# Windowed attention and an MLP in one kernel: the first two blocks of all four pairs of sequences first, the MLP in nine chunks of four blocks, v from the second block on by GpSimd's queue

## The chip, the cores and the metric

The kernel runs on one core of a Trainium2 chip. The metric is the device time of one execution in microseconds (us). The profile comes from one more such execution, in which the hardware recorded every instruction and every DMA packet; its times count from the start of its span.

## The reference

Attention over a window of 128 positions with a slope on the distance for each head, then a normalised two-layer MLP with a residual. Eight sequences of 576 positions, eight heads of 64, model width 512, hidden width 2048, all in float32:

```python
scores = scale * np.matmul(q, k.transpose(0, 1, 3, 2))
mask = (rel >= 0) & (rel < window)             # rel = position of q - position of k, window = 128
scores = np.where(mask, scores + bias[None], -1000000000.0)   # bias = -slope[head] * |rel|
attn = softmax(scores)
x = np.matmul(attn, v)                         # heads side by side: 8 x 576 x 512
xn = (x - mu) / np.sqrt(var + 1e-06) * g_ln
out = x + np.maximum(xn @ w_ch1, 0.0) @ w_ch2
```

## The kernel before

**Blocks.** The 8 x 576 positions are cut into 36 blocks of 128. Two sequences (a pair) make nine blocks (`PERIOD`); the middle one holds the end of one sequence and the start of the other. A block needs its own k and v and those of the block ahead of it in its pair; the first block of a pair (r = 0) needs only its own, and costs half. In the kernel before, block i is simply the i-th of the 36, so the four pairs follow each other.

**Attention of one block** (`attention(i)`). q and k come in as float32, are cast to fp16, turned so that the head dimension lies on the partitions (`qkt`), and multiplied (line 725, the tile `sc`, two halves of four heads each). ScalarE takes the exponential from `sc` into `probs` (773). For the first blocks (`i < BY_BIAS`) TensorE has added the slopes and the mask to `sc` beforehand, by multiplying `sid` with a table of distances (741); for the others VectorE multiplies `probs` with a table of masks (780), which ScalarE makes once (437). TensorE multiplies `probs` with `vx` (797); v has a column of ones, so the sums come with it. VectorE then does, in this order: reciprocal of the sums (814), `xb` = the normalised half (818) for both halves, the mean (851), `xs` = (xb - mean) * g (858), and the statistics (839, 845). `xs` is turned into `xt`, by TensorE (872, copied out by 880 or 882) for `i < X_BY_DMA` and by a transposing DMA on SP's queue (887) for the others.

**Three ways for q and k.** The blocks named in `SPANS` and the ones behind them come two at a time: one DMA on SP's queue (459) takes two positions at once, 512 bytes in a row, 1024 packets for the eight heads of two blocks; casts (619, 621) into `qs16`, `ks16`; four 32-bit transposes for each half of the heads (639); copies into `qkt` of both blocks (648, 650). `BY_HALVES` names the spans that are loaded and cast in two halves of four heads. Other early blocks come by 256-byte rows on SP's queue (364), and from `LOAD_CAST` on a DMA on GpSimd's queue casts on the way (473), and `qkt` is made by a transposing DMA on SP's queue (702) from `QK_BY_DMA` on. v of the blocks below `V_CAST` comes by SP's queue (364) and is cast by an engine (591, 593); from there on GpSimd's queue casts it on the way (473).

**MLP** (`mlp(c)`). The blocks are grouped in chunks; chunk c multiplies its `xt` with the first weights (919: 16 products `A` of four matmuls, as wide as the chunk has columns), applies relu (929, 931), and multiplies with the second weights (947: for each block 16 matmuls of 512 columns), then `ot` = product * rstd + xb (955) and out (963). The weights come in eight DMAs of 1 MB each on GpSimd's queue, casting: four for the first (536), four for the second (538). `W_AFTER` ties each to a point in the order of the loads.

**What sets the order.** A planner written in the kernel (`Plan.run`) lists all tasks with assumed costs and lays each on an engine by priority. The tables `PICK` (which engine), `PRI` (shifts of priority) and `HOLD` (earliest times) steer it. Its result is one fixed order of instructions on each engine and queue, and each engine works through its own in order; what the planner assumed does not hold anything back on the chip, only the order and the semaphores do. Where the planner sees TensorE idle before `WARM`, it fills the gap with matmuls on zeros (986) in whole numbers.

Rings (`Ring`) give the k-th user of a tile its buffer: buffer k modulo n, and the first write waits for the readers of user k - n.

Of the kernel before, what the change touches and what calls it, by code (L numbers as in the profile page):

```python
# [10 lines left out]
FP16 = mybir.dt.float16  # L11
# [15 lines left out]
class Ring:  # L27
    def __init__(self, tiles):
        self.tiles, self.first, self.readers = tiles, {}, {}

    def __getitem__(self, k):
        return self.tiles[k % len(self.tiles)]
# [7 lines left out]
    def link(self):  # L40
        n = len(self.tiles)
        for k, tasks in self.first.items():
            for t in tasks:
                t.deps += self.readers.get(k - n, [])


class Plan:
# [8 lines left out]
    LANDING = {"DMA SP": (0.7, 1.3), "DMA ACT": (0.7, 1.3), "DMA POOL": (2.1, 1.4)}  # L56
    LAST_OF_RUN = 1.0
# [6 lines left out]
    def ring(self, tiles):  # L64
        r = Ring(tiles)
        self.rings.append(r)
        return r
# [28 lines left out]
    def rates(self, queues):  # L96
        on = [q for q, x in queues.items() if x]
        if "DMA POOL" in on and len(on) > 1:
            a, b = (0.92, 0.17) if len(queues["DMA POOL"]) > 1 else (0.7, 0.4)
            return {q: a if q == "DMA POOL" else b / (len(on) - 1) for q in on}  # L100
        return {q: 1.0 / len(on) for q in on}
# [125 lines left out]
def kernel(  # L227
# [10 lines left out]
    nc = tc.nc  # L238
# [13 lines left out]
    CHUNKS = [3, 2, 3, 4, 4, 4, 4, 4, 4, 4]  # L252
# [15 lines left out]
    LEAD = 1.6  # L268
    WARM = 22.0
    TABLE_AFTER = 4  # L270
    STATS_LEAD = 10.0
    MIX_AFTER = 4
    SPLIT = 4
    LOAD_CAST = 9
    V_CAST = 5
    BY_HALVES = [0, 2, 5]
    HALVED = []
    SPANS = [0, 2, 5, 7]
    SLACK = (0, 0.2, 0)
    PICK = {('xt', 0): 'ACT', ('xt', 8): 'ACT DVE', ('cv', 5): 'ACT', ('cv', 0): 'POOL', ('ev', 8): 'ACT', ('ev', 1): 'DVE ACT', ('ev', 3): 'ACT', ('ck', 8): 'ACT', ('cq', 5): 'ACT', ('ev', 5): 'DVE', ('ck', 2): 'POOL', ('ck', 7): 'POOL ACT', ('cq', 6): 'POOL', ('cq', 2): 'POOL ACT', ('xt', 6): 'ACT', ('cq', 8): 'POOL', ('xt', 5): 'ACT', ('cv', 7): 'POOL ACT', ('cv', 3): 'ACT', ('xt', 3): 'DVE', ('ev00', 4): 'ACT', ('cs1', 1): 'POOL ACT', ('cs0', 0): 'POOL DVE', ('ev10', 3): 'ACT', ('xt', 2): 'DVE', ('cq', 3): 'POOL', ('cs0', 8): 'ACT', ('ev01', 8): 'DVE ACT', ('ev10', 8): 'DVE ACT', ('ev11', 5): 'ACT', ('cs0', 2): 'DVE', ('cq', 4): 'POOL', ('ev00', 8): 'DVE', ('ev01', 0): 'DVE ACT', ('cv', 8): 'POOL ACT', ('ev11', 0): 'ACT', ('cv', 4): 'POOL ACT', ('ev01', 6): 'ACT', ('cv', 6): 'POOL ACT', ('ev10', 5): 'ACT', ('cs1', 4): 'POOL', ('ev', 0): 'DVE', ('cv', 2): 'POOL ACT', ('ev00', 2): 'DVE ACT', ('ev00', 7): 'ACT', ('ev10', 2): 'ACT', ('xt', 1): 'ACT DVE', ('ev11', 8): 'DVE', ('xt', 4): 'DVE', ('ev00', 1): 'DVE ACT', ('cv', 1): 'POOL ACT', ('ev01', 7): 'DVE ACT', ('ev11', 6): 'DVE ACT', ('cq', 1): 'ACT', ('ev01', 4): 'DVE', ('cs0', 5): 'POOL', ('ev', 7): 'ACT', ('xt', 7): 'ACT DVE', ('ev', 9): 'ACT', ('cv', 9): 'POOL', ('cq', 11): 'POOL ACT', ('cs1', 9): 'POOL ACT', ('ev00', 10): 'ACT', ('eva', 5): 'ACT', ('cka', 9): 'ACT', ('cv', 11): 'POOL ACT', ('cqa', 10): 'DVE', ('ckb', 10): 'ACT', ('ck', 10): 'ACT', ('ev00', 5): 'ACT', ('ckb', 3): 'DVE', ('evb', 5): 'DVE', ('ev', 11): 'DVE', ('ev01', 2): 'DVE ACT', ('ckb', 6): 'ACT', ('eva', 11): 'DVE', ('cqb', 7): 'POOL DVE ACT', ('cka', 1): 'POOL DVE ACT', ('ev00', 3): 'ACT', ('cq', 0): 'ACT', ('ev01', 5): 'DVE', ('cqb', 5): 'DVE', ('ev10', 4): 'DVE ACT', ('ev01', 9): 'ACT', ('cqa', 8): 'ACT', ('ev10', 10): 'DVE', ('evb', 4): 'DVE ACT', ('cqb', 8): 'POOL ACT', ('cs0', 9): 'POOL DVE', ('cka', 3): 'POOL', ('cqa', 2): 'DVE', ('cka', 8): 'ACT', ('cqa', 5): 'POOL DVE ACT', ('cq', 7): 'POOL', ('ck', 1): 'POOL', ('cka', 0): 'POOL ACT', ('cqa', 7): 'ACT', ('ev10', 11): 'ACT', ('cqa', 4): 'ACT', ('ev11', 11): 'DVE', ('eva', 10): 'DVE ACT', ('ev11', 4): 'DVE', ('eva', 3): 'DVE', ('ev11', 2): 'DVE', ('cqa', 6): 'POOL', ('cqa', 9): 'POOL ACT', ('cqa', 11): 'POOL DVE ACT', ('ev', 2): 'DVE ACT', ('cs0', 4): 'POOL ACT', ('ckb', 11): 'DVE', ('ckb', 2): 'POOL DVE ACT', ('ck', 5): 'POOL', ('cs1', 8): 'ACT', ('ev01', 10): 'DVE ACT', ('ev', 10): 'DVE ACT', ('cq', 10): 'POOL', ('eva', 4): 'DVE', ('cv', 10): 'POOL', ('ev', 6): 'DVE ACT', ('ck', 11): 'ACT', ('cs1', 11): 'POOL ACT', ('cqb', 1): 'DVE', ('ckb', 7): 'DVE', ('ev11', 1): 'DVE ACT', ('ck', 4): 'POOL ACT', ('cka', 11): 'DVE', ('ckb', 0): 'POOL ACT', ('cs1', 0): 'POOL DVE', ('eva', 7): 'DVE', ('cs0', 11): 'POOL ACT', ('evb', 8): 'DVE ACT', ('ev10', 6): 'DVE', ('eva', 2): 'DVE', ('cqb', 2): 'ACT', ('cq', 9): 'POOL ACT', ('ev10', 9): 'DVE ACT', ('ev10', 0): 'DVE ACT', ('evb', 6): 'DVE ACT', ('eva', 8): 'ACT', ('cqa', 3): 'POOL ACT', ('ck', 9): 'ACT', ('evb', 3): 'DVE ACT', ('cs0', 1): 'DVE', ('cqb', 9): 'POOL DVE ACT', ('cqb', 0): 'POOL', ('evb', 2): 'ACT', ('evb', 1): 'ACT', ('cqb', 6): 'DVE', ('eva', 9): 'ACT', ('evb', 10): 'ACT', ('cqb', 11): 'DVE', ('cka', 10): 'POOL', ('ck', 6): 'POOL ACT', ('ckb', 1): 'POOL', ('ev10', 7): 'ACT', ('cs1', 7): 'ACT', ('ev01', 3): 'DVE', ('cs0', 7): 'POOL', ('cs0', 6): 'POOL DVE', ('cs1', 3): 'DVE', ('cka', 2): 'POOL ACT', ('cqa', 1): 'POOL ACT', ('ev01', 1): 'ACT', ('cs0', 10): 'POOL ACT', ('cka', 4): 'ACT', ('ev00', 6): 'DVE', ('xt', 10): 'DVE', ('cqb', 3): 'POOL DVE ACT', ('evb', 0): 'DVE ACT', ('ev00', 0): 'ACT', ('xt', 9): 'ACT', ('ev11', 7): 'DVE', ('cqb', 4): 'POOL DVE ACT', ('ev00', 9): 'DVE', ('ev00', 11): 'DVE ACT', ('ckb', 9): 'POOL ACT', ('ev11', 3): 'DVE ACT', ('ev01', 11): 'DVE', ('evb', 7): 'DVE ACT', ('ckb', 4): 'POOL ACT', ('ckb', 5): 'POOL ACT', ('cs1', 5): 'ACT', ('cs0', 3): 'POOL DVE', ('cka', 7): 'POOL', ('ev11', 9): 'DVE', ('cka', 5): 'ACT', ('cqb', 10): 'POOL', ('cs1', 6): 'POOL DVE', ('eva', 6): 'DVE', ('cs1', 10): 'POOL ACT', ('eva', 1): 'DVE', ('evb', 9): 'DVE ACT', ('ev10', 1): 'ACT', ('eva', 0): 'DVE', ('cka', 6): 'POOL ACT', ('ev11', 10): 'ACT', ('ev', 4): 'ACT', ('ck', 3): 'POOL ACT', ('cs00', 0): 'POOL ACT', ('cs10', 3): 'DVE', ('cs01', 10): 'ACT', ('cs11', 6): 'POOL', ('cs00', 9): 'POOL', ('cs01', 11): 'POOL', ('cs11', 9): 'ACT', ('cs00', 6): 'POOL DVE', ('cs11', 3): 'POOL DVE', ('cs01', 7): 'POOL', ('cs01', 8): 'POOL DVE', ('cs10', 11): 'POOL ACT', ('cs00', 8): 'DVE', ('cqa', 0): 'ACT', ('cs00', 2): 'POOL', ('cs01', 6): 'DVE', ('cs10', 4): 'DVE', ('cs10', 10): 'POOL ACT', ('cs00', 4): 'POOL', ('ck', 0): 'ACT', ('cs11', 5): 'DVE', ('cs11', 2): 'POOL', ('cs11', 8): 'DVE', ('cs01', 1): 'POOL', ('cs01', 4): 'POOL DVE', ('cs00', 1): 'POOL DVE', ('cs11', 0): 'POOL', ('ckb', 8): 'DVE', ('cs10', 9): 'POOL ACT', ('cs01', 9): 'POOL ACT', ('cs00', 10): 'POOL', ('cs01', 2): 'POOL', ('cs00', 5): 'POOL', ('cs11', 11): 'ACT', ('cs00', 3): 'POOL ACT', ('cs10', 1): 'ACT', ('cs01', 3): 'POOL', ('cs11', 1): 'DVE', ('cs11', 10): 'POOL DVE', ('cs11', 4): 'ACT', ('cs10', 6): 'POOL ACT', ('cs11', 7): 'ACT', ('cs10', 0): 'DVE', ('cs10', 5): 'ACT', ('cs10', 7): 'POOL'}  # L280
    PRI = {'T7.1': -4.2, 'A1.13': 6.1, 'rc0.8': -3.5, 'B4.0': 5.4}
    HOLD = {'mkb5': 43.12, 'v8.i': 46.02, 'nm0.7': 54.13, 'cT0.01': 7.07, 'cT5.10': 33.76, 'qs0.0.i': 1.25, 'g.i': 0.8, 'sid1': 4.85, 'mreg00': 28.48, 'z1': 31.56, 'r0.3': 28.11, 'r0.11': 36.69, 'rc1.8': 61.94}
    BY_BIAS = 5
    MASK_AT = 5
    QK_BY_DMA = 9
    X_BY_DMA = 12
# [7 lines left out]
    def ring(name, n, shape, dt):  # L294
        return plan.ring([sb(f"{name}{i}", shape, dt) for i in range(n)])
# [53 lines left out]

    def where(i):  # L350

        b0, r = 2 * (i // PERIOD), i % PERIOD
        if r < 4:
            return [(0, P, b0, P * r)]
        if r == 4:
# [23 lines left out]
    for t in vx.tiles:  # L379
        nc.vector.memset(t[:, :, D:VD], 1.0)  # L380
# [646 lines left out]
```

## Time and profile before

| | |
|---|---|
| Time, median of 8 executions (lowest, highest) | 320.58 us (319.49, 320.94) |
| The profiled execution: its time, its span | 320.02 us, 318.2 us |
| First matmul, end of the last | 1.07 us, 314.84 us |
| TensorE busy | 309.5 us, 2526 matmuls |
| of them the MLP's (lines 919 and 947) | 136.1 + 135.7 us, 640 + 592 |
| of them on zeros (line 986) | 8.0 us, 76 |
| VectorE, ScalarE, GpSimd busy | 185.5, 164.7, 98.7 us |
| First product of the MLP starts | 23.73 us |
| Landings of the four parts of the first weights | 22.09, 28.19, 34.94, 41.18 us |

A matmul's busy time is longer than the time that it keeps TensorE from the next, because matmuls overlap in the array. So work on TensorE is counted here by the time from one start to the next: 216 ns for 512 columns, 162 for 384, 109 for 256.

### The profile page before, as it was taken

What the parts mean: (1) busy time and instruction counts of PE and PEld (TensorE: products, weight loads), DVE (VectorE), ACT (ScalarE), POOL (GpSimd) and SP (SyncE); (2) the same over time, 40 slices, a digit from 0 to 9 for tenths busy, and PEclk for the clock granted to TensorE, in tenths of its full rate; (3) what the DMA queues carried; (4) which work ended last, traced back from release to release, by engine and by line L of the source; (5) the groups of instructions that cost most, each with busy time, mean ns of one, the idle gap of its engine ahead of it and who ended that gap; (6) DMA issues with size and microseconds to landing.
All of it is one profiled execution on the core that took longest, in us unless ns stands there. A gap on an engine that the chain in (4) does not pass through costs nothing.

```text
span 318.2 us, 6461 instructions
## 1 busy us (share of the span) xinstructions
PE 309.5 (97%) x2526; PEld 175.8 (55%) x2526; DVE 185.5 (58%) x511; ACT 164.7 (52%) x269; POOL 98.7 (31%) x131
## 2 busy tenths in 40 slices
PE   8988899999999999999999999999999999999995
PEld 7766676556655545554555555555555455445543
DVE  3679368865599648564866486548664866111012
ACT  2869776445656743474257425742575257305600
POOL 5746284674465346453533232001000000000000
PEclk9999999999999999999999999999999999999999
DMA  8999999999999999999999999628610221011011
GB/s 199 233 209 212 211 209 175 151 185 169 162 130 174 162 171 171 187 178 150 168 201 99 97 139 193 50 49 137 130 19 16 85 82 19 18 68 67 0 66 68
DMA packets 153906, 41.47 MB, mean 130 GB/s; under 512 B 138385, under 2 KB 148881, under 8 KB 153874
## 3 DMA queue, kind: packets, MB, share of 16 engines
q0 software_dynamic: 91232, 15.34, 70.4%
q1 hardware_dynamic: 62640, 25.70, 41.9%
q8 instruction: 20, 0.33, 0.5%
q14 instruction: 12, 0.10, 0.1%
q10 hardware_dynamic: 2, 0.00, 0.0%
HBM read 36.70 MB, written 9.44 MB: 145 GB/s over the span
## 4 chain that ended last, share of the span: by engine, by line
PE 86%; DMA 7%; SPq 5%; POOL 0%; issue 0%; DVE 0%; POOLq 0%
PE fb L947 40%; PE fb L919 36%; PE sc L725 5%; DMA w1sb<-in_moe_w_ch_dram 5%; PE fb L797 5%; SPq L364 3%; DMA qs<-in_q_dram 2%; SPq L459 2%; PE fb L872 1%; PE fb L639 0%; POOL vx L473 0%; POOL qs L621 0%; DVE ot L955 0%; POOLq L621 0%
## 5 line engine op out<-in xcount | busy, mean ns | idle before, releaser
L919 PE MATMUL fb<-xt,w1sb 128*128 128x512 f16 (+2 forms) x640 | 136.1, 359 | 1.7 <-DMA w1sb<-in_moe_w_ch_dram 1.7
L947 PE MATMUL fb<-w2sb,ht 128*128 128x512 f16 (+2 forms) x592 | 135.7, 373 | 0.0
L931 ACT ACTIVATE ht<-fb 128x512 f16<-128x512 f32 (+2 forms) x145 | 80.9, 560 | 63.2 <-PE fb L919 61.9
L773 ACT ACTIVATE probs<-sc 128x1024 f16<-128x1024 f32 (+1 forms) x72 | 67.6, 973 | 55.0 <-PE sc L725 55.0
L919 PEld LDWEIGHTS <-w1sb 128*128 128x128 f16 x640 | 68.2, 114 | 48.9 <-DMA w1sb<-in_moe_w_ch_dram 2.6
L947 PEld LDWEIGHTS <-ht 128*128 128x128 f16 x592 | 54.1, 98 | 56.9
L955 DVE SCALAR_TENSOR_TENSOR ot<-fb,rstd,xb 128x512 f32<-128x512 f32 (+2 forms) x37 | 27.2, 736 | 53.9 <-PE fb L947 53.6
L473 POOL DMA_DIRECT2D vx<-in_v_dram x34 | 28.8, 849 | 74.0 <-PE fb L797 59.0
L780 DVE TENSOR_TENSOR probs<-probs,mreg 128x1024 f16<-128x1024 f16 (+1 forms) x48 | 31.4, 657 | 28.5 <-ACT probs L773 28.2
L797 PEld LDWEIGHTS <-probs 128*128 128x128 f16 x544 | 25.4, 98 | 14.0 <-ACT probs L773 0.3
L818 DVE SCALAR_TENSOR_TENSOR xb<-fb,rec 128x256 f16<-128x256 f32 x72 | 30.5, 423 | 2.0
L473 POOL DMA_DIRECT2D qk<-in_q_dram x30 | 25.4, 847 | 17.6 <-DMA qkt<-qk 6.3
L473 POOL DMA_DIRECT2D qk<-in_k_dram x30 | 25.3, 844 | 11.6 <-DMA qk<-in_k_dram 4.7
L797 PE MATMUL fb<-vx,probs 128*128 128x65 f16 x544 | 28.4, 193 | 0.0
L858 DVE SCALAR_TENSOR_TENSOR xs<-xb,mean,g_t 128x512 f16<-128x512 f16 x36 | 27.5, 763 | 0.9 <-DMA xt<-xs 0.2
L839 DVE BATCH_NORM_STATS2 st<-xb 128x6 f32<-128x512 f16 x36 | 24.6, 685 | 0.0
L814 DVE RECIPROCAL rec<-fb 128x4 f32<-128x4 f32 x72 | 13.0, 180 | 18.4 <-PE fb L797 17.7
L725 PEld LDWEIGHTS <-qkt 64*128 64x128 f16 x544 | 15.3, 94 | 12.3 <-issue 10.5
L725 PE MATMUL sc<-qkt 64*128 64x128 f16 x288 | 19.7, 216 | 0.0
L725 PE MATMUL sc<-qkt,qkt 64*128 64x128 f16 x256 | 18.4, 219 | 0.0
L929 DVE TENSOR_SCALAR ht<-fb 128x384 f16<-128x384 f32 (+2 forms) x15 | 8.5, 566 | 6.4 <-PE fb L919 5.5
L650 ACT ACTIVATE qkt<-fb 128x512 f16<-128x512 f16 x10 | 5.6, 597 | 7.5 <-PE fb L639 7.0
(62 smaller groups left out, 123.9 us busy)
## 6 DMA issues: line engine op xcount, KB each, us to landing
out_dram<-ot SPq DMA_DIRECT2D x35, 256.0 KB, 3.5
vx<-in_v_dram POOLq DMA_DIRECT2D x28, 128.0 KB, 9.9
qk<-in_q_dram POOLq DMA_DIRECT2D x24, 128.0 KB, 11.2
qk<-in_k_dram POOLq DMA_DIRECT2D x24, 128.0 KB, 10.9
w1sb<-in_moe_w_ch_dram POOLq DMA_DIRECT2D x4, 512.0 KB, 11.4
w2sb<-in_moe_w_ch_dram POOLq DMA_DIRECT2D x4, 512.0 KB, 13.0
ks<-in_k_dram SPq DMA_DIRECT2D x6, 256.0 KB, 4.7
qs<-in_q_dram SPq DMA_DIRECT2D x6, 256.0 KB, 5.2
```

The lines of the kernel that those rows point to most:

```text
L473: nc.gpsimd.dma_start(out=dst(p0, n), in_=src[b, :, s0 : s0 + n, :].rearrange("h p d -> p h d"))
L725: nc.tensor.matmul(scs[half][:, g, c0 : c0 + P], kt[rows, 1, hp, :], qkt[i][rows, 0, hp, :], start=not bias, stop=True, skip_group_check=True,
L773: nc.scalar.activation(out=o, in_=n_, func=AF.Exp, scale=inv_sqrt_d)
L780: en.tensor_tensor(out=pv, in0=pv, in1=mask[:, 2 * half : 2 * half + 2, :, lo:], op=ALU.mult)
L797: nc.tensor.matmul(pp[:, hh * (D + 1) : hh * (D + 1) + D + 1], probs[i][:, bank, slot, side * P : side * P + P], vx[i - 1 + side][:, h, 0 ...
L818: nc.vector.scalar_tensor_tensor(out=xb[i][:, 256 * half : 256 * half + 256].rearrange("p (h d) -> p h d", d=D), in0=pp[:, :, 0:D], scalar ...
L839: nc.vector.bn_stats(out=st[i][:, :], in_=xb[i][:, :])
L858: nc.vector.scalar_tensor_tensor(out=xs[i][:, :], in0=xb[i][:, :], scalar=mean[i][:, 0:1], in1=g_t[:, :], op0=ALU.subtract, op1=ALU.mult,)
L919: nc.tensor.matmul(fb[b][:, 0:n_], w1f[f // CB][:, kb, f % CB, :], xt[c][:, kb, 0:n_], start=(kb == 0), stop=(kb == NKB - 1),)
L931: nc.scalar.activation(out=ht[c][:, f, 0:n_], in_=src, func=AF.Relu)
L947: nc.tensor.matmul(pm[:, 0 : c1 - c0], ht[c][:, f, j * P : j * P + P], w2sb[f // CB][:, f % CB, c0:c1], start=(f == 0), stop=(f == NFB - 1),)
L955: nc.vector.scalar_tensor_tensor(out=ot[i][:, c0:c1], in0=fb[plan.held[key][1]][:, 0 : c1 - c0], scalar=rstd[c][:, j : j + 1], in1=xb[i][: ...
```

## The change

The order of the blocks changes: `BLOCK` lists first the blocks 0 and 1 of each of the four pairs, then the rest. In the following, block i is the i-th in this new order: 0 and 1 are the first pair's, 2 and 3 the second pair's, up to 7; 8 is then block 2 of the first pair. All of blocks 0 to 7 come as spans. The second block of each pair has to keep its k and v until block 2 of its pair is done, so `qkt` and `vx` get four buffers of their own (`pins`, at the places `FAR` = 1, 3, 5, 7), outside of the rings.

```diff
+        return self.pins[k] if k in self.pins else self.tiles[self.turn(k) % len(self.tiles)]
...
-    CHUNKS = [3, 2, 3, 4, 4, 4, 4, 4, 4, 4]
+    CHUNKS = [4, 4, 4, 4, 4, 4, 4, 4, 4]
...
-    LEAD = 1.6
-    WARM = 22.0
-    TABLE_AFTER = 4
+    LEAD = 1.5
+    WARM = 20.0
+    TABLE_AFTER = 5
...
-    MIX_AFTER = 4
-    SPLIT = 4
-    LOAD_CAST = 9
-    V_CAST = 5
-    BY_HALVES = [0, 2, 5]
+    MIX_AFTER = 9
+    SPLIT = 6
+    LOAD_CAST = 8
+    V_CAST = 1
+    BY_HALVES = [0, 4]
...
-    SPANS = [0, 2, 5, 7]
-    SLACK = (0, 0.2, 0)
+    SPANS = [0, 2, 4, 6]
+    SLACK = (0, 0.8, 0.1)
...
-    BY_BIAS = 5
-    MASK_AT = 5
-    QK_BY_DMA = 9
-    X_BY_DMA = 12
+    HEADS = 4
+    BY_BIAS = 6
+    MASK_AT = 6
+    QK_BY_DMA = 11
+    X_BY_DMA = 6
...
+    BLOCK = [b for n in range(HEADS) for b in (PERIOD * n, PERIOD * n + 1)]
+    BLOCK += [b for b in range(NBLK) if b not in BLOCK]
+    PLACE = {b: i for i, b in enumerate(BLOCK)}
+    FAR = [i for i, b in enumerate(BLOCK) if b + 1 < NBLK and (b + 1) % PERIOD and PLACE[b + 1] > i + 1]
...
-    qk16 = ring("qk16", 6, [P, 2, d_model], FP16)
-    vx = ring("vx", 7 if V_CAST > 4 else 9, [P, H, VD], FP16)
-    qkt = ring("qkt", 6, [P, 2, HP, P], FP16)
+    qk16 = ring("qk16", 5, [P, 2, d_model], FP16)
+    vx = ring("vx", 7 if V_CAST > 4 else 9, [P, H, VD], FP16, FAR)
+    qkt = ring("qkt", 6, [P, 2, HP, P], FP16, FAR)
...
-        b0, r = 2 * (i // PERIOD), i % PERIOD
+        b0, r = 2 * (BLOCK[i] // PERIOD), BLOCK[i] % PERIOD
...
-    W_AFTER = [6, 12, 17, 18, 21, 22, 22, 28]
+    W_AFTER = [9, 12, 12, 14, 16, 19, 22, 23]
...
-        r = i % PERIOD
+        r = BLOCK[i] % PERIOD
+        before = PLACE[BLOCK[i] - 1] if r else None
...
-                nc.sync.dma_start(out=out_flat[i * P : i * P + P, c0:c1], in_=ot[i][:, c0:c1])
+                nc.sync.dma_start(out=out_flat[BLOCK[i] * P : BLOCK[i] * P + P, c0:c1], in_=ot[i][:, c0:c1])
```

Wherever the block ahead was `i - 1`, it is now `before`. The tables `PICK`, `PRI` (4 entries before, over 150 now) and `HOLD` are new, and some of the planner's assumed costs change (a table `SHARES` for how two queues share the DMA engines, some landing times). The rest follows from the order that comes out of it. How the changed kernel's queues and engines begin, w0 to w3 being the four parts of the first weights, and q, k, v with the number of their block (or of the span's first):

```
SP      q0 first half, k0 first half, q0 second half, v0, k0 second half, q2 (both blocks, all heads), k2 (the same),
        k4 first half, k4 second half, q4 first half, q4 second half, q6, k6, then the x of block 6 by transposing DMA
GpSimd  distances, identity, two masks, load v1, one mask, load v2, distances, load v3, load w0, load v4,
        cast k4 first half, load w1, load w2, cast q4 first half, load w3, cast q4 second half, load v5,
        cast q6, then the loads of w4, v6, w5, v7, w6, w7 (w4 to w7: second weights), q8, v8, k8, v9 ...
ScalarE cast q0 first half, cast v0, cast k0 second half, cast q0 second half, exp of block 0 first half, g,
        exp of block 0 second half, cast k2, exp of block 1 (two halves), exp of block 2 first half ...
VectorE ..., cast k0 first half, two copies to qkt, cast q2, two copies to qkt, block 0's normalisation, then (31 in all):
        copies to qkt of blocks 2 and 3, the normalisation of blocks 1, 2, 3 and half of 4, and two copies to xt;
        the last of these is block 3's xt
TensorE 34 matmuls on zeros, slopes of block 0, 42 on zeros, transposes of span 0 first half, 10 on zeros ...
        transposes of span 2, ..., up to the slopes of block 5; then the first product A of chunk 0
```

On TensorE the counts change so: slopes (741) 48 matmuls instead of 40; transposes for `xt` (872) 24 instead of 48; transposes of fp16 q and k (687) 24 instead of 8; matmuls on zeros 95 instead of 76; the first products of the MLP 576 of 512 columns instead of 448 of 512, 128 of 384 and 64 of 256. All other counts are the same. The loads of v change from six on SP and 34 on GpSimd's queue to one and 39 (some blocks take two); SP no longer loads q and k by 256-byte rows.

## The prediction

> **What bounds the kernel now.** I read first the busy shares, then TensorE's waits, the chain of waits in order of time, then the loads with their landings and VectorE's groups.
>
> ```profile
> PE 309.5 (97%) x2526; PEld 175.8 (55%) x2526; DVE 185.5 (58%) x511; ACT 164.7 (52%) x269; POOL 98.7 (31%) x131
> ...
> PE fb L919 <- DMA w1sb<-in_moe_w_ch_dram: 1.7, 2, 1.1
> PE fb L687 <- POOL qk L560: 1.3, 1, 1.3
> ...
> 25.61 15.58 DMA w1sb<-in_moe_w_ch_dram
> 41.18 0.05 issue
> 41.23 2.14 PE fb L919 x12
> ```
>
> TensorE is the bound, and the chain is TensorE alone from 41.23 us on; ahead of that it is the load of the last part of the first weights, issued at 25.61. So a change can win or lose only in the first 41 us, and I count TensorE's work there. Per matmul, start to start in the trace: 216 ns for 512 columns, 162 for 384, 109 for 256, 107 for the slopes, 109 for the float32 transposes, 56 for the others, 35.5 for line 725 (19.3 us over 544), 31.5 for line 797 (17.1 over 544), and 1.05 us for g. Over all matmuls but those on zeros this makes 297.3 us. At 41.23 us 26.6 of it is done: 14.6 us are lost by then (late start, zeros, waits). The stretch from there to the last matmul loses 3.0 more, and 3.4 lie behind it (314.84 to 318.2): 297.3 + 14.6 + 3.0 + 3.4 = 318.3, the span. I call "loss" at a point the clock less the work done; the largest loss that any wait forces sets the end.
>
> **Work.** Slopes +8 x 0.107, transposes of xs -24 x 0.056, of q and k +16 x 0.056: +0.4, total 297.7. The chunks of 2 and 3 blocks cost nothing extra before (109 and 162 ns are 256 and 384 columns at the rate of 512), so nine even chunks win nothing. Of these 297.7 us, 14.0 stand ahead of the first product A of chunk 0, in the new order, and 4.7 ahead of the transposes of span 2.
>
> **Moved: v1, v2, v3 and w0 go ahead, beside SP's queue.** These are the rows for a load:
>
> ```profile
> vx<-in_v_dram POOLq DMA_DIRECT2D x28, 128.0 KB, 9.9
> w1sb<-in_moe_w_ch_dram POOLq DMA_DIRECT2D x4, 512.0 KB, 11.4
> ks<-in_k_dram SPq DMA_DIRECT2D x6, 256.0 KB, 4.7
> v<-in_v_dram SPq DMA_DIRECT2D x4, 256.0 KB, 5.7
> ```
>
> The first two land about 10 us after issue because both queues feed the same 16 DMA engines. Counting the trace's packets by queue and size in each microsecond: SP alone moves 570 of 512 bytes (3 to 5 us) or 850 of 256 (6 to 7, 12 to 14). Together they go one for one: a v of GpSimd's queue (128 bytes written) and 512-byte packets 318 each (28, 34 us), with 256-byte packets 380 each (58 us), a weight (1024 bytes) and 512-byte packets 140 each (31 us). In the kernel before, w0 was issued at 14.76, and SP was alone until 16.8.
>
> Now the sum for k2, the last load that span 2 needs. SP queues 512 (q0), 512 (k0), 512 (q0), 1024 (v0), 512 (k0), 1024 (q2), 1024 (k2) packets: 5120. They start at 1.95. v1 is issued after GpSimd's 1.1 us of tables (from 0.81), at 1.9; w0's first packet came 2.06 after its issue, so v1's come at 4.0. SP alone: 2.05 x 570 = 1170. Then v1: 366 / 318 + 658 / 380 = 2.9; v2: 366 / 380 + 658 / 318 = 3.0; v3: 1024 / 318 = 3.2; w0: 512 / 140 = 3.7. At 16.8 SP has moved 1170 + 3584 = 4754; the other 366 go beside v4 in 1.15. Last packet 17.9, landing 0.45 later (v and w land 0.35 to 0.45 after theirs): 18.4. Bounds: if the two queues didn't hinder each other, 1.95 + 4096 / 570 + 1024 / 850 + 0.45 = 10.8; the sum itself is the other end. I take 18.4, as the pairs were measured with these very packets. In the kernel before, the same data, by halves, were there at about 13.
>
> The Trainium skill, page "DMA: Bandwidth & Descriptors", section "Anatomy of one DMA — SWDGE (gpsimd) path", speaks for less: such a load moves at 436 GB/s behind a fixed 2 us. By that, an estimate, three v and w0 take 4.2 us of the engines, k2 lands near 15, and the change would cost nothing; the measured pairs say twice that.
>
> **The wait that this makes.** ScalarE's cast of k2 stands ahead of the exponentials of blocks 1 to 3. Half a span takes 0.78 on ScalarE, the whole 1.33 on GpSimd; I take 1.4: 19.8. TensorE's transposes of span 2 wait for it, with block 1's line 797 behind them. The k transposes and the latency to VectorE take 0.4: the first copy starts at 20.15. From there VectorE has 31 instructions in order, the last being the xt that A of chunk 0 waits for:
>
> ```profile
> L818 DVE SCALAR_TENSOR_TENSOR xb<-fb,rec 128x256 f16<-128x256 f32 x72 | 30.5, 423 | 2.0
> L858 DVE SCALAR_TENSOR_TENSOR xs<-xb,mean,g_t 128x512 f16<-128x512 f16 x36 | 27.5, 763 | 0.9 <-DMA xt<-xs 0.2
> L839 DVE BATCH_NORM_STATS2 st<-xb 128x6 f32<-128x512 f16 x36 | 24.6, 685 | 0.0
> L814 DVE RECIPROCAL rec<-fb 128x4 f32<-128x4 f32 x72 | 13.0, 180 | 18.4 <-PE fb L797 17.7
> L851 DVE TENSOR_SCALAR mean<-sums 128x1 f32<-128x1 f32 x36 | 7.6, 212 | 1.1
> L845 DVE BATCH_NORM_AGGREGATE mv<-st 128x2 f32<-128x6 f32 x36 | 6.3, 176 | 0.8
> L648 DVE COPY qkt<-fb 128x512 f16<-128x512 f16 x6 | 2.5, 412 | 6.4 <-ACT qkt L650 4.8 <-PE fb L639 1.6
> ```
>
> (Columns: busy us, mean ns of one, idle time before.) Whole durations: 7 x 0.423 + 7 x 0.083 (the accumulator's read after each) + 3 x 0.763 + 3 x 0.685 + 7 x 0.180 + 3 x 0.212 + 2 x 0.176 + 6 x 0.415 (four copies to qkt, two to xt) = 12.6; back to back they start closer (0.35, 0.67, 0.60, 0.09, 0.17, 0.12, 0.33), 9.6. Dependent steps (reciprocal to 818, to mean, to xs) keep nearly the whole duration, independent ones overlap; I take the middle, 11.1. So A starts at 20.15 + 11.1 + 0.15 = 31.4, at a loss of 31.4 - 14.0 = 17.4. TensorE's own work from span 2 to A is 14.0 - 4.7 = 9.3 us and lies under VectorE's 11.1.
>
> **What is hidden.** GpSimd's cast of k4 holds w1 and w2 until 20.8, that of q4 holds w3 until 23. By the rates, k4 lands at 20 and q4 at 22 and 22.9; w1, w2, w3, beside q6 and k6 at 140 packets each, land near 27, 30.5 and 34, k6 at 35, v5 at 36.5. TensorE wants them at 17.4 plus the work ahead of each: w1 at 34.0, w2 at 36.8, v5 at 39.4, k6 (after a cast of 0.8) at 40.1, w3 at 43.4. So the old wait for the last weights is gone, by 9 us, and pays nothing. If A came early, v5 would be the next: 36.5 - 22.0 work = 14.5. The second weights follow at 2.5 us each (44.52, 46.94, 49.41 before), the loads of v at 0.9: w7 lands near 49, wanted at 56. The 34 + 42 + 10 zeros cost nothing on the path: TensorE's pitch drops from 107 to 56 ns at 6.3 us, so they end near 8.2. q2 lands at 13.1, and VectorE's cast of it (0.8) stands ahead of the copies for block 0's second half; four copies, slopes, scores and one exponential later, at 16.5, TensorE is at span 2, whose k is not there. The fewer 780 and cast instructions on VectorE and GpSimd lie beside this.
>
> While it waits from 16.5 to 19.8 TensorE is idle for 3.3 us. The longest idle time of the trace before is 1.3 us (at 21.39), and the pitch stayed at 56 ns. The Trainium skill, page "TensorE: Matmul & The Clock Gate", section "What's actually happening", says that an idle window of about 3.4 us halves the clock until 3.4 us of work have passed. By that, an estimate, 1.7 us more of TensorE's time go beside VectorE's 11.1 us, and up to 0.5 shows. Neither is in the sum.
>
> **Sum.** 297.7 work + 17.4 loss + 3.2 (3.0 as before, 0.2 as A starts 10 us sooner in the count) + 3.4 behind = 321.7 against 318.2: +3.5. The profiled execution was 320.02, the median 320.58; I add to the median: 324.1, say 324.0.
>
> **Rivals.**
> 1. A further wait comes on top (slower, 325.5). Blocks 6 and 7 turn their x by DMA now, and chunk 1's first A waits for them. Block 7's line 797 is at 34.5 of work, 52.3 us, xs some 1.9 later, so the DMA is issued at 54.3. Transposing DMAs took 7.4 to 9.9 us from issue while GpSimd's loads were running (4.7 in the median over all); they run until about 61. It lands between 61.7 and 64.2; TensorE is there at 44.7 + 17.4 + 0.6 = 62.7. For: the slow ones all lie in that load. Against: the margin at 8 us. With 9.9 it costs 64.2 - 62.7 = 1.5 us: 325.5.
> 2. SP keeps its rate, and k2 lands by 13.5 (faster, 319.1). Place: the start of SP's queue; v1 to v3 and w0 would have to cost SP less than 2.7 us instead of 7.5. Then A starts at 13.5 + 1.75 + 11.1 + 0.15 = 26.5, loss 12.5; v5 has to land by 34.5 too, as the earlier casts would let it. 297.7 + 12.5 + 3.2 + 3.4 = 316.8, -1.4: 319.1. It decides from k2 at 15 down: there A is at 28, and the loss is 14. For: the SP queue issues first, and what it frees is real (w3 at 34 instead of 41). Against: the one-for-one packets.
> 3. The change doesn't do what it says: k2 lands near 15, and v5 or the span of blocks 6 and 7 forces the loss of 14 to 14.6 that w3 forced before: 320.6. For: w3's gap of 9 us is not won where v5 is wanted. Against: k2 as above.
>
> **How the numbers follow.** The forecast 324.0 has 0.55 (its own range 322.5 to 325.5, for VectorE's 9.6 to 12.6), rival 1 0.25, rival 2 0.13, rival 3 0.07. What a measurement of this kernel can tell from no change is 0.2%, 0.6 us. So slower 0.80, same 0.07, faster 0.13. The range goes down to 320.2, leaving out rival 2, and up to 327.0, for VectorE's 12.6 instead of 11.1 (1.5) with rival 1.
>
> **What would show it.** Right: in the changed profile k2 lands near 18, TensorE's longest wait stands at its transposes at about 17 to 20 us, chunk 0's first A starts near 31.4, VectorE is gapless before it, and no wait for the weights is left. Wrong: A starts before 28.5, or a wait for a load appears after 40 us; or TensorE's matmuls at 56 ns go at 107 after the wait.

## The result, and the profile after

The changed kernel takes 324.44 us in the median of 11 runs (322.43 to 325.47), the kernel before 320.39 (319.49 to 321.32, 32 runs): a ratio of 1.0122, 95% interval 1.0107 to 1.0137. The profiled execution, which took 324.44 itself, has a span of 322.6 us against 318.2.

From the page of the changed kernel: the span, each engine's busy time, TensorE's granted clock in 40 slices of 8.07 us (tenths of full speed), and the chain by engine and line. Line numbers are now the changed kernel's: 483 SP's loads of the spans, 618, 646 and 648 casts, 666 the transposes of the spans, 675 and 677 the copies to `qkt`, 750 the scores, 822 the product with v, 839 the reciprocal, 843 xb, 864 the statistics, 883 xs, 897 the transposes of xs, 944 the first product A of the MLP, 972 the second.

```profile
span 322.6 us, 6345 instructions
...
PE 311.7 (97%) x2481; PEld 171.4 (53%) x2481; DVE 191.6 (59%) x522; ACT 157.8 (49%) x243; POOL 97.7 (30%) x129
...
PEclk9979999999999999999999999999999999999999
...
PE 91%; DMA 4%; DVE 2%; SPq 1%; ACT 0%; issue 0%
PE fb L944 39%; PE fb L972 39%; PE sc L750 5%; PE fb L822 5%; DMA ks<-in_k_dram 4%; SPq L483 1%; DVE xs L883 1%; PE fb L666 1%; DVE xb L843 1%; PE sc L766 0%; ACT ks L646 0%; PE fb L714 0%; PE fb L897 0%; DVE rec L839 0%; DVE st L864 0%
```

The load of k2 (4% is 13 us) has taken the place of w1's last part in the chain. The third slice of the clock (16.1 to 24.2 us) is 0.7; before, it was full from 6.3 us on. TensorE's waits (us in total, times, longest):

```profile
PE fb L666 <- ACT qs L646: 2.7, 1, 2.7
PE fb L666 <- ACT ks L646: 2.5, 1, 2.5
PE fb L897 <- DVE xs L883: 1.2, 2, 1.0
```

No wait for weights is left. There are two waits at transposes instead: the first, ahead of TensorE's very first transposes (T0.1, at 11.44 us), for the cast of q0's second half; the second, at 20.00, for the cast of k2.

T0.0 and T0.1 are the transposes of the two halves of span 0's heads. In TensorE's order T0.1, the second half, comes first, and not the first half, as the list under "The change" has it. The loads that T0.1 needs had landed at 4.51 (k) and 6.90 us (q). But ScalarE works in order, and there the cast of that half of q stands behind the cast of v0 (landed at 8.97) and that of the other half of k0 (9.98), neither of which T0.1 needs (start us, us):

```profile
8.99 0.63 ACT L618 ACTIVATE vx<-v 128x512 f16<-128x512 f32 x1 [4.61 <-DMA v<-in_v_dram]
10.00 0.77 ACT L646 ACTIVATE ks<-ks 128x512 f16<-128x512 f32 x1 [0.38 <-DMA ks<-in_k_dram]
10.64 0.74 ACT L646 ACTIVATE qs<-qs 128x512 f16<-128x512 f32 x1
```

So the first wait has two causes: late loads, and a new order of casts that makes the first transposes wait for them. The chain from k2 to the first A (start us, us, what):

```profile
5.62 12.96 DMA ks<-in_k_dram
...
18.61 1.34 ACT ks L646
...
20.00 0.89 PE fb L666 x6
...
25.37 1.84 DVE xs L883
...
32.90 3.61 PE fb L944 x16
```

k2 is issued at 5.62 and lands at 18.58. The first A starts at 32.90, with 14.0 us of work ahead of it: a loss of 18.9 us against 14.6 before. That 4.3 is the difference of the spans, 4.4. Behind A the trace has nothing new: 2.65 us are lost there. In the profiles of the change and of all its variants below, the span ends 289.65 to 289.71 us after the first A starts. So all that these kernels win or lose, they win or lose ahead of the first A; to reach the span of the kernel before, 318.2, A would have to start at 28.5.

Now the clock. The same trace, cut at multiples of 3.41 us counted from the moment at which the clock came up (7.08 us); columns: window, TensorE busy us (instructions), granted clock, DMA share, GB/s.

```profile
7.08:10.49 3.41, 1.70 (x30) 1.00 1.53 250
10.49:13.91 3.42, 2.47 (x25) 1.00 1.47 206
13.91:17.32 3.41, 3.41 (x44) 1.00 1.34 212
17.32:20.73 3.41, 0.87 (x8) 1.00 1.26 289
20.73:24.14 3.41, 3.41 (x40) 0.50 1.15 290
```

The window that holds the second wait is busy for 0.87 us, and the whole next one runs at half clock. The first wait, 2.7 us, is cut in two by the border at 10.49 and does nothing to the clock here. It doesn't seem to fall so in most executions: of the twelve with a recorded mean clock, seven had 0.982 to 0.984 (323.95 to 325.47 us), one 0.988 (322.96), three 0.995 (322.85 to 324.44) and one 1.000 (322.43). One window at half clock is 1.7 of some 320 us, 0.5% of the mean: by this most executions lost three windows, the profiled one a single one. None of those with three was profiled, so what they do has to be taken from the profiles of the variants. The count of windows doesn't give the time alone: the execution with two took 322.96, one of those with a single window 324.44. And the kernel before isn't free of it: of the 57 executions of it that ran beside the variants, 38 had a mean clock of 0.995 or less, in the median 320.44 us against 320.21 for the others.

### The profile page after: what moved, and what is told of

Read it like the earlier page. It is cut to its first block, busy times and chain, and to the rows that moved or that the text cites. A ratio compares the mean times of both kernels' runs of the same rounds, so it can differ in the third digit from the quotient of the medians.

```text
span 322.6 us, 6345 instructions
## 1 busy us (share of the span) xinstructions
PE 311.7 (97%) x2481; PEld 171.4 (53%) x2481; DVE 191.6 (59%) x522; ACT 157.8 (49%) x243; POOL 97.7 (30%) x129
## 4 chain that ended last, share of the span: by engine, by line
PE 91%; DMA 4%; DVE 2%; SPq 1%; ACT 0%; issue 0%
PE fb L944 39%; PE fb L972 39%; PE sc L750 5%; PE fb L822 5%; DMA ks<-in_k_dram 4%; SPq L483 1%; DVE xs L883 1%; PE fb L666 1%; DVE xb L843 1%; PE sc L766 0%; ACT ks L646 0%; PE fb L714 0%; PE fb L897 0%; DVE rec L839 0%; DVE st L864 0%
## 5 line engine op out<-in xcount | busy, mean ns | idle before, releaser
L944 PE MATMUL fb<-xt,w1sb 128*128 128x512 f16 x576 | 134.1, 380 | 0.0
L972 PE MATMUL fb<-w2sb,ht 128*128 128x512 f16 (+2 forms) x592 | 132.0, 373 | 0.0
L956 ACT ACTIVATE ht<-fb 128x512 f16<-128x512 f32 x128 | 76.5, 598 | 84.6 <-PE fb L944 82.9
L944 PEld LDWEIGHTS <-w1sb 128*128 128x128 f16 x576 | 61.7, 114 | 51.1
L499 POOL DMA_DIRECT2D vx<-in_v_dram x35 | 30.3, 868 | 47.5 <-PE fb L822 44.7
L805 DVE TENSOR_TENSOR probs<-probs,mreg 128x1024 f16<-128x1024 f16 (+1 forms) x44 | 29.8, 679 | 22.0 <-ACT probs L798 21.8
L839 DVE RECIPROCAL rec<-fb 128x4 f32<-128x4 f32 x72 | 12.2, 177 | 25.3 <-PE fb L822 25.3
L750 PEld LDWEIGHTS <-qkt 64*128 64x128 f16 x480 | 14.6, 94 | 11.7 <-issue 9.1
L750 PE MATMUL sc<-qkt 64*128 64x128 f16 x256 | 17.8, 219 | 0.0
L750 PE MATMUL sc<-qkt,qkt 64*128 64x128 f16 x192 | 13.6, 219 | 0.0
L954 DVE TENSOR_SCALAR ht<-fb 128x512 f16<-128x512 f32 x16 | 11.1, 692 | 2.9 <-PE fb L944 2.8
L1011 PE MATMUL fb<-warm_t 128*128 128x128 f16 x95 | 9.1, 270 | 1.1 <-DVE warm_t L400 1.1
```

The lines of the kernel that those rows point to most:

```text
L499: nc.gpsimd.dma_start(out=dst(p0, n), in_=src[b, :, s0 : s0 + n, :].rearrange("h p d -> p h d"))
L750: nc.tensor.matmul(scs[half][:, g, c0 : c0 + P], kt[rows, 1, hp, :], qkt[i][rows, 0, hp, :], start=not bias, stop=True, skip_group_check=True,
L805: en.tensor_tensor(out=pv, in0=pv, in1=mask[:, 2 * half : 2 * half + 2, :, lo:], op=ALU.mult)
L944: nc.tensor.matmul(fb[b][:, 0:n_], w1f[f // CB][:, kb, f % CB, :], xt[c][:, kb, 0:n_], start=(kb == 0), stop=(kb == NKB - 1),)
L956: nc.scalar.activation(out=ht[c][:, f, 0:n_], in_=src, func=AF.Relu)
L972: nc.tensor.matmul(pm[:, 0 : c1 - c0], ht[c][:, f, j * P : j * P + P], w2sb[f // CB][:, f % CB, c0:c1], start=(f == 0), stop=(f == NFB - 1),)
```

## The experiments

Edits are to the changed kernel. Most move a task in the list of the order in which instructions are issued, with this helper behind the planner's run:

```
+    def move(name, behind):
+        at = next(n for n, x in enumerate(order) if x[0].name == name)
+        task = order.pop(at)
+        order.insert(next(n for n, x in enumerate(order) if x[0].name == behind) + 1, task)
```

`cT4.10` is GpSimd's cast of half of k4, the first of its instructions that waits for a load of SP's; what stands behind it is issued only when that half has landed.

**w0 later.**

```
+    move('w0.i', 'cT4.10')
```

> The changed kernel with one issue moved: the load of w0 stands behind GpSimd's first cast (that of half of k4) instead of ahead of it; all else is the same. My theory (the loads on GpSimd's queue hold back k2, and k2 sets the end): w0's 512 packets no longer go beside k2's last 530; v4's do, at 318 a microsecond instead of 140, so k2 lands near 16.3 us instead of 18.58, TensorE's wait at its transposes shrinks from 2.5 to some 0.5 us, the first A starts 2.2 us sooner (30.7), and the time falls by about 2.2 us to 322.2. w0 itself lands near 25, well ahead of A. Rival (k2's landing is not what sets the end: VectorE's backlog or a later wait does): k2 lands sooner and the time stays at 324.0 to 324.6.

323.86 us (322.65 to 325.31, 6 runs), ratio 1.0112, 1.0086 to 1.0138: not told apart from the change. k2 landed at 16.57 as expected, but the 2.2 us did not come. Its waits say why:

```profile
PE fb L666 <- ACT qs L646: 3.8, 1, 3.8
...
PE sc L750 <- DVE qkt L675: 0.4, 1, 0.4
```

A wait for k2 (by ScalarE's cast of ks) is no longer in the list; next in it are 0.4 us. The first wait is 3.8 us, and behind it the clock was 0.50 from 13.33 to 20.16 (two windows), so that TensorE itself came to span 2 only at 20.80. In such an execution k2 isn't what is late.

**q6's cast later.**

```
+    move('cT6.00', 'w7.i')
```

> The changed kernel with GpSimd's cast of q6 moved behind its last weight issue (w7), so that it no longer runs beside VectorE's xs of block 1 at 25.3 us. Theory (the cast slows the fp16 VectorE instruction beside it: 1.90 us for xs instead of 0.75): that xs takes 0.75 to 0.8, the first A starts about 1.1 us sooner (31.8 instead of 32.90) and the time falls by some 1.1 us to 323.3. Rival (xs is slow for another reason, such as the state of its tiles, or VectorE has slack there): xs stays near 1.9, or A does not move, 324.4.

324.11 us (322.65 to 325.03, 6 runs), ratio 1.0117, 1.0095 to 1.0138: no gain shown. In its profile the first A started at 31.97 us, as the theory had it (31.8), but the clock was halved elsewhere (12.94 to 16.36) and TensorE came to span 2 three microseconds later, so this A isn't to be compared with 32.90. The xs of block 1 fell from 1.90 to 1.09 us, for now it met another cast. These are VectorE's xs and GpSimd's casts in the timeline of the changed kernel (start us, us):

```profile
17.27 0.75 DVE L883 SCALAR_TENSOR_TENSOR xs<-xb,mean,g_t 128x512 f16<-128x512 f16 x1
25.32 1.90 DVE L883 SCALAR_TENSOR_TENSOR xs<-xb,mean,g_t 128x512 f16<-128x512 f16 x1
...
25.35 1.36 POOL L648 CAST qs<-qs 128x1024 f16<-128x1024 f32 x1
```

and the xs of block 1 with the cast beside it in this experiment:

```profile
25.19 1.09 DVE L883 SCALAR_TENSOR_TENSOR xs<-xb,mean,g_t 128x512 f16<-128x512 f16 x1
...
24.98 0.80 POOL L648 CAST qs<-qs 128x512 f16<-128x512 f32 x1
```

An xs beside a cast ends 0.5 us after the cast's end in both (27.22 and 26.71; 26.28 and 25.78), and in the kernel before too (13.41 and 12.92). So the cast makes it longer. What that costs at the end this run doesn't show, but three profiles below, in which VectorE is idle for at most 0.13 us between the k transposes of span 2 and A, do: with all xs of blocks 1 to 3 at 0.72 to 0.75 us A came 10.61 and 10.62 us after these transposes (the fourth and the third kernel with 46 zeros), with an xs of 1.71 beside a cast 11.30 us (the first). By this, an estimate, a cast beside an xs costs A some 0.7 us.

**Zeros in the second wait.**

```
             if e == "PE":
+                if t.name == "T2.0":
+                    for _ in range(44):
+                        nc.tensor.matmul(fb[b][:, 0:P], warm_t[:, :], warm_t[:, :], start=True, stop=True)
```

> The changed kernel with 44 matmuls on zeros in TensorE's wait ahead of the transposes of span 2 (17.0 to 19.5 us), so that the engine isn't idle while k2 is late; no load or cast is moved. Theory (the idle time halves TensorE's clock: the granted clock was 0.50 from 20.1 to 24 us, and line 822's matmuls came every 54 ns instead of 31): the granted clock stays at 1.00, line 822 goes at 31 ns from 20.9 us on, and the first A starts 0.5 to 1.4 us sooner, 323.0 to 323.9. Rival (VectorE alone bounds this stretch, TensorE's halved clock is hidden beside it): the clock stays up, A moves by 0.3 us at most, 324.1 to 324.5.

325.17 us (323.82 to 327.17, 6 runs), ratio 1.0161, 1.0130 to 1.0192: 0.7 above the change in the median, though the intervals touch, and outside both theories. Its profile is an execution with three windows at half clock:

```profile
9.08:12.49 3.41, 0.65 (x7) 1.00 1.54 233
12.49:15.90 3.41, 3.41 (x22) 0.50 1.27 215
15.90:19.32 3.42, 3.42 (x26) 0.50 1.36 247
19.32:22.73 3.41, 3.41 (x33) 0.50 1.01 272
```

Most of the first wait (3.7 us, 8.10 to 11.84) fell into one window. Why the clock then stayed at half for three windows, though TensorE was busy in them, is open. TensorE was late at span 2, there was no second wait to fill, and the 44 zeros, 3.35 us from 21.19 on, stood in the way: the first A at 35.15. This is where a new theory came from: the first wait, through the clock, makes most executions slow.

**Only v1 ahead.**

```
+    move('v2.i', 'cT4.10')
+    move('v3.i', 'v2.i')
+    move('v4.i', 'v3.i')
+    move('w0.i', 'v4.i')
```

> The changed kernel with v2, v3, v4 and w0 all moved behind GpSimd's first cast, so that only v1 goes beside SP's first loads. My theory (packets of the two queues go one for one, so each load of GpSimd's that goes ahead costs k2 its own packets' time): k2 lands near 12.5 us, six us sooner; then v2 and v3 (near 17.5 and 19) hold blocks 2 and 3, the first A starts near 28, and the loads that were pushed back (w3, v5, now 35 to 38) become the wait that counts, at a loss near 16 instead of 18.9: 321.5 to 322.5. Rival (the queues share in another way, and k2 is late by its own queue): k2 lands at 17 or later, and the time stays at 324 or grows.

322.37 us (319.76 to 323.93, 12 runs), ratio 1.0060, 1.0033 to 1.0087: in the range of my theory, and k2 landed at 12.94 (12.5 expected). But the time fits for another reason. What came next was not the weights: TensorE reached span 2 at 19.48, again because of the first wait (3.0 us) and two windows at half clock. The first A started at 30.53, not 28. The two executions with a mean clock of 0.999 took 319.76 and 319.95, less than the median of the kernel before (320.35 beside it).

**46 zeros, in the wrong place.** I meant to fill the first wait, and put them ahead of T0.0. In TensorE's order T0.1 comes first, so they stood behind the wait. The second of the four kernels also has the 44 zeros ahead of T2.0, the third w0 later, the fourth only v1 ahead:

```
+                for _ in range({'T0.0': 46}.get(t.name, 0)):
+                    nc.tensor.matmul(fb[b][:, 0:P], warm_t[:, :], warm_t[:, :], start=True, stop=True)
```

> The changed kernel with 46 more matmuls on zeros ahead of TensorE's very first transposes (T0.0), where it waited 2.66 us in the profile of the changed kernel and 3 to 4.7 us in the profiles of its variants; they end near 10.8 us, and T0.0 starts at 10.9 to 12.3 anyway. No load, cast or wait moves. New theory (what most executions lose is the clock that this first wait halves: granted 0.50 from about 12.5 us until 16 to 22 us in four profiles, and the changed kernel's executions with a mean clock of 0.982 to 0.984 took 324.0 to 325.5 us, those of 0.995 and more 322.4 to 324.4): the clock stays at 1.00 until the second wait, and the time falls to 322.4 to 323.3. Rival (my prediction's own theory: k2's landing alone sets the first A, and a halved clock ahead of it is hidden): 324.2 to 324.6, unchanged.

> As the kernel with 46 zeros ahead of T0.0, with 44 more ahead of the transposes of span 2 (from about 17.0 to 19.5 us, while k2 is not there). New theory (each idle time of 2.5 us or more halves the clock for 3.3 us or a multiple): the granted clock is 1.00 from start to end, line 822 goes at 31 ns after 20 us, and the first A starts 0.5 to 1.4 us sooner than with the first zeros alone: 321.6 to 322.8. Rival (VectorE bounds the stretch behind span 2, the clock there is hidden): the same time as with the first zeros alone, within 0.3 us.

> As the kernel with 46 zeros ahead of T0.0, with the load of w0 behind GpSimd's first cast, so that k2 lands near 16.5 us (measured) instead of 18.6. New theory (w0's place won nothing by itself, 323.86, only because the halved clock brought TensorE to span 2 at 20 us, later than k2; with the clock up, k2 decides as the prediction had it): 1.5 to 2.2 us faster than with the zeros alone, 320.3 to 321.6. Rival (k2's landing doesn't set the first A in any case): no faster than with the zeros alone, within 0.4 us.

> As the kernel with 46 zeros ahead of T0.0, with v2, v3, v4 and w0 all behind GpSimd's first cast (only v1 beside SP's first loads). By itself this order took 322.37 in the median, but 319.8 to 319.95 in its two executions with a mean clock of 0.999. New theory (the two losses, the halved clock and the shared queue, add up): nearly all executions stand at the lower end, 319.6 to 320.4, with a spread of less than 1.5 us. Rival (the spread has another cause, such as the landing of the loads): the median stays above 321.5.

326.05, 327.60, 324.39 and 323.59 us (ratios 1.0155, 1.0200, 1.0102 and 1.0085). None of them tests what it was meant for; the intervals are 0.003 to 0.005 wide to each side. What they do show is a delay given to TensorE alone: 46 zeros took 3.05 us from 14.47 on in the first, span 2 came at 21.50, and the first A at 33.07, though k2 had landed at 18.87. With k2 at 16.26 (the third) it was span 2 at 21.77 and A at 32.67. ScalarE's cast of k2, which stands behind block 0's exponentials in its order, was late with TensorE there: it ended at 21.51 and 21.77. Whoever comes last to span 2, k2 or TensorE, sets A, 10.5 to 11.3 us after the k transposes in the profiles where TensorE is last. The fourth happened to have the clear case for the windows: a first wait of 2.88 us (8.67 to 11.55) across a border, and no loss of clock.

```profile
6.86:10.27 3.41, 1.81 (x32) 1.00 1.21 287
10.27:13.69 3.42, 2.14 (x32) 1.00 0.93 254
13.69:17.10 3.41, 3.41 (x44) 1.00 0.95 258
```

**56 zeros in the first wait.**

```
+                for _ in range({'T0.1': 56}.get(t.name, 0)):
+                    nc.tensor.matmul(fb[b][:, 0:P], warm_t[:, :], warm_t[:, :], start=True, stop=True)
```

> The changed kernel with 56 more matmuls on zeros ahead of TensorE's true first transposes (T0.1 comes first in its order; the earlier 46 stood behind that wait, at 13 to 15 us, and only made TensorE later). They fill the first wait, from about 8.2 to 11.4 us. Theory (the halved clock behind the first wait costs most executions some 1 to 2 us): the granted clock is 1.00 until the second wait at 17 us, and the median falls to 322.4 to 323.6, near the executions of the changed kernel with a mean clock of 0.995 and more (322.4 to 324.4). Rival (k2's landing at 18.6 sets the start of span 2 with either clock): 324.1 to 324.7.

323.30 us (322.48 to 324.84, 6 runs), ratio 1.0094, 1.0067 to 1.0121: where the theory put it, though the interval overlaps that of the change. What the zeros alter is how often the clock falls: three of six executions had a mean clock of 1.000 (322.48 to 322.80), against one of twelve (322.43); at 1.000 and 0.995 the times are near those of the change (322.43; 322.85 to 324.44). The profile has 1.00 until 21.71; the second wait then halves one window, as it did in the profile of the change.

**The same, with w0 later.** Both edits together.

> As the kernel with 56 zeros ahead of T0.1, with the load of w0 behind GpSimd's first cast, so that k2 lands at 16.3 to 16.6 us (measured in two runs) instead of 18.6. Theory (with the clock up TensorE reaches span 2 at 17 us, and k2 decides): the transposes of span 2 end at 18.3 instead of 20.9, the second wait is too short to halve the clock, the first A starts near 30, and the time is 2 us below that with the zeros alone: 320.3 to 321.7. Rival (k2's landing doesn't set the end): within 0.4 us of the kernel with the zeros alone.

321.22 us (320.46 to 323.45, 12 runs), ratio 1.0021, 1.0002 to 1.0040: 2.1 us below the zeros alone, intervals apart. It is also 2.6 us below w0 later alone (1.0086 to 1.0138), intervals apart again: so beside this order of loads the zeros themselves, which move no load, are shown to win. The same move that won nothing shown by itself wins its expected two microseconds once the clock stays up: k2 landed at 17.15, the k transposes began at 18.57 instead of 20.03, and the first A at 30.29 instead of 32.22. Eleven of twelve executions had a mean clock of 0.998 or more; their median of 321.19 is 1.3 us below the three executions at 1.000 with the zeros alone (median 322.49). By this, an estimate, some 1.3 of the 2.1 us are k2's earlier landing at an equal clock, and the rest is the clock. Its waits:

```profile
PE fb L666 <- ACT qs L646: 1.5, 1, 1.5
...
PE fb L897 <- DVE xs L883: 1.0, 2, 0.8
```

**Nothing ahead.**

```
+    move('v1.i', 'cT4.10')
+    move('v2.i', 'v1.i')
+    move('v3.i', 'v2.i')
+    move('v4.i', 'v3.i')
+    move('w0.i', 'v4.i')
```

> The changed kernel with v1, v2, v3, v4 and w0 all behind GpSimd's first cast: nothing of GpSimd's queue runs beside SP's first loads; chunks, spans and casts stay as changed. Theory (both waits of the changed kernel are made by the loads put ahead): k0's second half lands near 7.2 us instead of 10.0, the first transposes start near 8.7 with no idle time over 1.5 us, the clock stays at 1.00, k2 lands near 10.5 and span 2 starts at 14 to 15; block 1 then waits about 1 us for v1 (landing near 16), the first A starts at 26.5 to 28, and v5 and the weights, pushed back by some 5 us, decide at a loss of 13.6 to 14.5: 319.0 to 320.3. Rival (what costs time are the parts that stay, the nine chunks and the new order of casts): still above 322.

321.77 us (321.16 to 324.81, 12 runs), ratio 1.0050, 1.0029 to 1.0071. Below the change by 2.7, intervals apart, but 1.5 above the range that I gave. k0's second half landed at 8.28 instead of 9.98, the first wait fell to 1.9 us, and span 2's transposes went at 15.3 without a wait. So the second wait of the change was made by the loads put ahead. The first they only made longer: 1.9 us of it stay, where the kernel before waits 0.4 us at its second transposes (8.64 us) and not at all at its first (5.84). Here too T0.1's q had landed early, at 6.28, and was cast at 8.95 only, behind v0 and k0's other half. And a new wait is there:

```profile
PE fb L822 <- DMA vxp<-in_v_dram: 2.2, 1, 2.2
PE fb L666 <- ACT qs L646: 1.9, 1, 1.9
```

v1, issued at 13.68, needs 4.9 us beside SP's other loads and lands at 18.60, not near 16. Block 1 waits for it, in one window, and that halves the next; the first A starts at 30.08, not at 26.5 to 28:

```profile
15.36:18.77 3.41, 1.21 (x16) 1.00 1.52 178
18.77:22.19 3.42, 3.42 (x40) 0.50 1.76 211
```

**Nothing ahead, v5 before w3.** The same with `move('v5.i', 'w2.i')`.

> As the kernel with nothing ahead, with v5 also moved ahead of the last part of w1 (w3) on GpSimd's queue. Theory (once the first A comes early, v5 is the next load that decides, as the prediction had it: its landing less 22.0 us of work): v5 lands some 2.5 us sooner, and the loss that counts falls to that of w1 and w2, 12.7 to 13.3: 0.5 to 1.0 us below the kernel with nothing ahead, 318.3 to 319.5, under the kernel before. Rival (the first A or the first weights decide): within 0.3 us of the kernel with nothing ahead.

322.32 us (321.18 to 323.44, 7 runs), ratio 1.0057, 1.0038 to 1.0077: not faster, which speaks for the rival, though the median is 0.55 above nothing ahead instead of within 0.3 (the intervals overlap). v5 landed at 31.37 instead of 34.91, and nothing had waited for it; v1's wait was 2.8 us in this profile and cost two windows (18.31 to 25.14). The first A, not a later load, decides.

No version ran faster than the kernel before in the median. Not tried: only v1 ahead together with zeros at the true first wait; the cast of q0's second half ahead of those of v0 and k0 on ScalarE, which would move no load; the nine chunks by themselves; and which of v1, v2, v3 costs how much.

## Why the prediction was right, and where it was not

- **k2 waits in the shared queues: right.** Predicted landing 18.4, measured 18.58; cast 1.4, measured 1.34. The packets of both queues one for one gave it. They also gave 16.3 without w0 (16.57 measured) and 12.5 with v1 alone (12.94). For v1 behind k4 they were used too lightly: 16 expected, 18.60 measured. That 18.4 came so close is in part luck: in the six profiles whose queues are the same up to k2, it landed at 18.58, 18.61, 18.87, 19.45, 19.78 and 20.08.
- **The second wait: right in its place** (17 to 20 us), and with the clock up k2 does set the end: 2.1 us for an earlier k2, some 1.3 of them at an equal clock.
- **"31 VectorE instructions, 11.1 us": mis-sized.** From 20.47 to the end of the xt at 32.85 it took 12.4. One xs took 1.90 beside a cast instead of 0.763, and VectorE had idle time behind a TensorE at half clock. A came at 32.9, not 31.4. From k transposes to A, the profile with zeros and w0 later, all at full clock, took 11.7; the two with one window at half clock behind the wait took 12.2 (zeros alone) and 12.9 (the change). With zeros alone no xs of blocks 1 to 3 met a cast; in the other two one took 1.90. With 0.7 us for that, an estimate from the profiles with 46 zeros, some 11.0 are left at full clock without such a cast. So the sum was near for an undisturbed stretch (11.6 from the k transposes at 19.8 to A at 31.4), and what it lacked were the cast beside xs and the clock.
- **"Neither is in the sum" (the clock): the step that failed.** I looked for an idle time over 3.4 us, found one of 3.3, and let up to 0.5 show. In 3.41 us windows 2.1 us of idle time and more were enough each time, and once 1.7. What it costs isn't up to 0.5: by the stretches above, 12.2 us with one window at half clock against some 11.0 without, it is about 1.2, an estimate. It is the larger of the two terms by which A came later than predicted; the cast beside xs, some 0.7, is the other, and wasn't in the sum at all.
- **"At 16.5 TensorE is at span 2": right for the profiled execution (17.0), probably not for most.** I priced k2 and didn't ask what the same packets do to the loads ahead of it. k0's second half lands at 9.98 (8.28 with nothing ahead), and by ScalarE's order of casts TensorE waits 2.7 to 4.7 us for its first transposes, without zeros in that wait; I had the zeros end at 8.2 and no wait behind them. Where that halves the clock, TensorE comes to span 2 late: at 19.5 to 21.2 us in the first four variants' profiles, in three of them after k2's cast was done. So where the median agrees with me, it is partly for another reason, and partly luck: for the profiled execution, which went the way that I forecast, the sum was 0.9 us too low.
- **Later losses:** 3.2 predicted, 2.65 measured. Together: A 1.5 later than predicted, 0.55 less after it, hence a span of 322.6 for 321.7.
- **Hidden loads: right.** w1, w2, w3 at 28.7, 31.3, 33.8, v5 at 34.65, w7 at 46.2; nothing waited for them, and the old wait for weights paid nothing.
- **Rivals.** 1: chunk 1's x by transposing DMA landed at 58.75 and 61.88, ahead of TensorE at 63.8; it didn't happen. 2 and 3: k2 at 18.58 rules them out. That v5 would be next if A came early was not so in the run made for it: A came at 30.08 and 31.41 there, too late to test the forecast for an A near 26.5.

What is left open: the change stands 4.05 us above the kernel before. Zeros in the first wait took 1.1 of that (intervals overlap), w0 behind the cast 2.1 more. The last 0.8 wasn't split: VectorE's stretch, the loads of v that remain ahead and the 1.5 us that TensorE still waits for its first transposes all stand there. With nothing ahead 1.35 us above the kernel before (320.42 beside it) stay: the wait for v1, the order of casts and the nine chunks stand there, not split either.

## What to carry to other kernels

A load put ahead on a second queue took turns here, packet by packet, with every load that was still in the first: price each of them, not only the last one wanted, and ask which instructions stand behind each on the engine that waits for it. A wait of TensorE of some 2 us can cost more than its length, since it may put the next 3.4 us at half clock; and whether it does can change from one execution to the next, so look at the mean clock of all executions before trusting one profile. If undoing a part alone wins nothing, try it together with what may hide it.

## What the runs showed of the hardware

- The clock changed only on a grid of 3.41 us. Between the first and the last product, all stretches at half clock in the profiles of the change and its variants were 3.41, 6.83 or 10.24 us long, and the grid lay anew in each execution (the clock first came up between 4.65 and 7.08 us). The Trainium skill, page "TensorE: Matmul & The Clock Gate", section "What's actually happening", has this free-running window of 3413 ns, and the traces agree. It says that an idle window halves the clock; here windows with 0.65 to 1.29 us of work did so too. The border is near half: 1.70 us busy kept the clock (the change, 7.08 to 10.49) and 1.73 lost it, as the line below from the kernel with zeros in the first wait shows. So the busy time, as the profile counts it, doesn't settle the border. Which rule holds stays open, and so does why some stretches lasted two or three windows though TensorE was busy in them.

```profile
18.30:21.71 3.41, 1.73 (x26) 1.00 1.24 298
21.71:25.13 3.42, 3.42 (x38) 0.50 1.16 226
```

- VectorE's xs (two fp16 inputs from SBUF) takes 0.75 us alone and up to 1.90 beside a GpSimd cast, ending 0.5 us after it. In the profile with zeros and w0 later, a cast that began during an xs took 1.14 instead of 0.76. The Trainium skill, page "SBUF — State Buffer", section "SBUF: two separate sides", says that the two share a port that one instruction holds to its end, also for a VectorE instruction with two SBUF inputs against a GpSimd one that reads SBUF. These rows agree that one of the two waits. They don't show that the one that starts first goes first: the xs of 1.90 us is recorded from 25.32 and the cast from 25.35, and the xs was the one made longer.
